# Holding w_out and moving g in a fused attention and two-MLP kernel on one Trainium2 core, with three shifts of side work

## The chip, the cores and the metric

One core of a Trainium2 (trn2) chip runs the whole program; the other cores are idle. The metric is the device time of one execution in microseconds. TensorE is written PE in the profile, and its weight loads PEld; VectorE is DVE, ScalarE is ACT, GpSimd is POOL, and SP is the engine whose queue issues nearly all DMAs.

## The reference

Attention with keys and values pooled by eight, then a gated MLP, then an MLP with a squared ReLU:

```python
k_p = k.reshape(B, H, Sp, 8, D).mean(axis=3); v_p = v.reshape(B, H, Sp, 8, D).mean(axis=3)
x = softmax(q @ k_p.T / sqrt(D)) @ v_p          # 8 x 8 heads, 576 queries, 72 pooled keys, D = 64
x = x.transpose(0, 2, 1, 3).reshape(4608, 512)
x = ((x @ w1) * (x @ w2)) @ w3 @ w_out1         # 512 -> 1024 -> 1024 -> 512
g = maximum(x @ w_in, 0) ** 2                   # 512 -> 2048
out = g @ w_out                                 # 2048 -> 512, float32
```

The inputs and weights are 8-byte floats in memory, and the kernel joins the two words of each weight into a float32.

## The kernel before, in words

Every product is made in three passes: each operand is split in a high and a low fp32r part (`hi` by ACT, `lo` by DVE), and high x high, high x low and low x high are added in PSUM. The program has these stages.

- **Fold** (`fold`): w3 @ w_out1 is folded into one matrix `W`, in groups of rows of w3. Beside it, attention tasks begin, called from `tick`, which stands between matmuls and runs a list of pumps. One pump is `attend`, the attention itself; another, `load_back`, loads k, v and q in pieces.
- **First MLP** (`stage_ab`, `stage_w`): nine blocks of 512 tokens, interleaved with the attention of later tokens. The first 512 columns of w1 and w2 stay in SBUF (`wt`). The second 512 columns are prepared by `second_half` (load, join, `hi`, `lo`, four stores), kept in a DRAM scratch as units of 256 KB (`u_w`) and fetched again for each block through a ring of eight tiles (`un`, `fetch`, L222). The pump `feed_w12` runs one step of that preparation at each tick; it is put on the list after the fold, and `stage_ab(0, 3)` waits until all steps have been issued.
- **Second MLP in pairs of blocks**: blocks are taken two at a time by a 2x2 block scheme with seven products in place of eight (Strassen's, in Winograd's form). An `h_step` (224 of them: 4 pairs x 8 units x 7 products) makes x @ w_in: six matmuls 128x512, a weight unit `un` held and the split x moved (`x2o`). An `o_step` (224 as well) makes g @ w_out. Before, it holds 128 tokens of the split g (`gt`) and moves 256 columns of w_out: twelve matmuls 128x256. The sums of an `o_step`'s product `m` are gathered in PSUM (`ob`) over eight units `u`, then added into SBUF tiles at the last unit; after products 3, 4, 5 and 6 one quarter of the pair's output is complete and is stored (`finish`, `store_out`).
- **Last block**: `ph_step` (16) and `po_step` (16) make the ninth block without the seven-product scheme.

The order of h and o steps is written by `plan`: the h steps of a pair are interleaved with the o steps of the pair before it, after a head of twelve o steps alone (`HEAD`), with a count of SBUF slots for g (`SLOTS`, `MORE`). `o_prep` splits g for an o step three o steps ahead, and it may also first replace g by a difference of two g's (L1026); the `gt` tiles are three buffers, so the split for o step k begins when o step k - 3 is done. The x of the next pair is split by `operands_of`: seven closures `cut` (B11, T1, T2, T3, B21, B22, T4, in this order; the T's with a subtraction first), which the main loop calls at marked steps (`todo_x`). The engines' final order is set by a scheduler at build time, and each engine then runs its own list in order.

The quarters of the weights w_in and w_out (`make_quarters`) are made once beside the first MLP and kept as units in DRAM.

Of the kernel before, what the change touches and what calls it, by code (L numbers as in the profile page):

```python
# [29 lines left out]
def attn_moe_moe2_kernel(  # L30
# [560 lines left out]
    def fold():  # L591
# [143 lines left out]

    def make_quarters(load, put_part):

# [12 lines left out]
        def sums(half):  # L750
            w = st_["w"]
            if half == 0:
                st_["s"] = prep_p.tile([P, 2, TB], F32, tag="w", name="sq")
            s_ = st_["s"]
            a11, a21 = w[:, 0, :PC], w[:, 0, PC:]
            a12, a22 = w[:, 1, :PC], w[:, 1, PC:]
            if half == 0:
                nc.vector.tensor_add(s_[:, 0, :PC], a21, a22)
                nc.vector.tensor_sub(s_[:, 0, PC:], s_[:, 0, :PC], a11)  # L759
            else:  # L760
                nc.vector.tensor_sub(s_[:, 1, :PC], a11, a21)
                nc.vector.tensor_sub(s_[:, 1, PC:], a12, s_[:, 0, PC:])

# [6 lines left out]
        def hi(n):  # L770
            st_["o", n] = t = prep_p.tile([P, 2, TB], F32R, tag="w", name="oq")
            nc.scalar.copy(t[:, 0, :], part(n))

        def lo(n):
            t = st_["o", n]
            nc.vector.tensor_sub(t[:, 1, :], part(n), f32(t[:, 0, :]))

# [14 lines left out]
    def in_quarters(kd, c):  # L792
# [13 lines left out]

        return make_quarters(load, put_part)

    def out_unit(key):
        return key.rearrange("p a b c -> p (a b c)").rearrange("p (i c) -> p i c", i=2)  # L810

    def out_quarters(u):
# [4 lines left out]
        return make_quarters(  # L817
            lambda x: load64(w_out[(u + x * NU) * P:(u + x * NU + 1) * P, :], raw_p), put_part)

# [17 lines left out]


    SLOTS, MORE = 38, 8

# [10 lines left out]
    def plan():  # L851
# [3 lines left out]
        free = [SLOTS]  # L855
        rest = [0]

        def out_step(todo):
            _, p, m, u = step = todo.pop(0)
            seq.append(step)  # L860
            free[0] += m in (2, 4, 5, 6)
            if u == NU - 1:
                new = (2, 2, 4, 0, 0, 0, 0)[m]
                free[0] += (0, 0, 0, 2, 2, 2, 2)[m] - new
                rest[0] -= new
            assert free[0] >= 0

        for p in range(len(pairs) + 1):
            todo = [("o", p - 1, m, u) for m in range(7) for u in range(NU)] if p else []
            if p == 1:  # L870
                free[0] += MORE
            rest[0] = 8 if p else 0
            n_o = len(todo)
# [7 lines left out]
            for x, step in enumerate(hs):  # L881
                need = step[0] == "ph" or step[3] >= 3
                while free[0] - rest[0] < need:
                    out_step(todo)
# [145 lines left out]

    def store_out(t, blk, x, half):

        r0 = blk * TB + x * 2 * P
        nc.sync.dma_start(
            out[r0:r0 + 2 * P, half * PC:(half + 1) * PC].rearrange("(t p) c -> p t c", p=P),
            t.rearrange("p (t c) -> p t c", t=2))

    def o_step(p, m, u):
# [4 lines left out]
        gt = gts.pop(("o", p, m, u))  # L1043
        for o in range(NT_):
            ps = ob[x][o // 2][:, o % 2 * PC:(o % 2 + 1) * PC]
            os_ = slice(o * P, (o + 1) * P)
            todo = [(gt[:, 0, os_], un[:, 0]), (gt[:, 0, os_], un[:, 1]), (gt[:, 1, os_], un[:, 0])]
            for j, (l, r) in enumerate(todo):
                nc.tensor.matmul(  # L1049
                    ps, l, r, start=u == 0 and m != 5 and o % 2 == 0 and j == 0,  # L1050
                    stop=u == NU - 1 and j == 2,
                    skip_group_check=True)
        fetch()
# [7 lines left out]

        def new(name, src, b):
            t = take((name, b))
            nc.vector.tensor_add(t, ob[x][b], gs[src, b])

        def add(name, b):
            nc.vector.tensor_add(gs[name, b], ob[x][b], gs[name, b])

        def finish(name, b, blk, half):
            add(name, b)  # L1070
            store_out(gs[name, b], blk, b, half)
            drop((name, b))

        for b in range(2):
            if m == 0:
                nc.scalar.copy(take(("x1", b)), ob[x][b])
            elif m == 1:
                new("x5", "x1", b)
            elif m == 2:
                new("x7", "x1", b)  # L1080
                new("x8", "x5", b)
            elif m == 3:
                add("x7", b)
                finish("x8", b, iB, 1)
            elif m == 4:
                finish("x7", b, iA, 1)
            elif m == 5:
                finish("x5", b, iB, 0)
            else:
                finish("x1", b, iA, 0)  # L1090

    def po_step(i, u):
# [6 lines left out]
        for o in range(NT_):  # L1099
# [8 lines left out]
            if u == U2 - 1:  # L1108
                st = tmp_p.tile([P, DM], F32, tag="cg", name="st2", bufs=3)
                if o % 2:  # L1110
                    nc.vector.tensor_copy(st, acc[o])
                else:
                    nc.scalar.copy(st, acc[o])
                r0 = i * TB + o * P
                nc.sync.dma_start(out[r0:r0 + P, :], st)
# [4 lines left out]
    def start_attention():  # L1120
# [3 lines left out]
        rate[0] = 0.7  # L1124


    setup_consts()
    fold()
    until(lambda: tokens_ready(TB))
    rate[0] = 0.6  # L1130

    def second_half(nm_, w, kc):
# [18 lines left out]
        def put():  # L1151
            for u in range(TB // P, U1):
# [5 lines left out]
    fh1 = merge([second_half(nm_, w, kc) for nm_, w in (("w1", w1), ("w2", w2))  # L1158
                 for kc in range(KD)], 2)
    feeds = []  # L1160
    second = []

    def feed_w12():
        if fh1:
            run_step(fh1)

# [18 lines left out]
    rate_q = [3]  # L1185
    pumps.extend([feed_w12, feed_quarters, begin_second, feed_operands])
    for i in range(NB):
# [47 lines left out]

    halves(more)
    for _ in range(U1):
# [19 lines left out]
    for step in order:  # L1257
        if step[0] == "h":
# [16 lines left out]
        else:  # L1275
            if step[:3] == ("o", 0, 0) and step[3] == 0:
                while quarters:
                    run_step(quarters)
                for _ in range(MORE // 2):
                    halves(prep_p.tile([P, 2, TB], F32, tag="w", name="gs"))  # L1280
# [39 lines left out]
```

## Time and profile before

| | us |
|---|---|
| median of 3 runs (1600.09 to 1604.88) | 1601.07 |
| the profiled execution, its own time | 1605.63 |
| its span in the profile | 1603.8 |
| PE busy in the span | 1531.9 (96%) |
| DVE busy | 975.5 (61%) |
| ACT busy | 786.4 (49%) |

The profile's page gives busy times of whole engines, the span in 40 equal slices (40.1 us each) with a digit for the busy tenths, the DMA queues, and the chain of work that ended last. A busy time is an average over stages: what a change in one stage is worth is read in that stage. The span is 1.8 us shorter than the profiled execution's own time.

### The profile page before, as it was taken

What the parts mean: (1) busy time and instruction counts of PE and PEld (TensorE: products, weight loads), DVE (VectorE), ACT (ScalarE), POOL (GpSimd) and SP (SyncE); (2) the same over time, 40 slices, a digit from 0 to 9 for tenths busy, and PEclk for the clock granted to TensorE, in tenths of its full rate; (3) what the DMA queues carried; (4) which work ended last, traced back from release to release, by engine and by line L of the source; (5) the groups of instructions that cost most, each with busy time, mean ns of one, the idle gap of its engine ahead of it and who ended that gap; (6) DMA issues with size and microseconds to landing.
All of it is one profiled execution on the core that took longest, in us unless ns stands there. A gap on an engine that the chain in (4) does not pass through costs nothing.

```text
span 1603.8 us, 24613 instructions
## 1 busy us (share of the span) xinstructions
PE 1531.9 (96%) x8288; PEld 1285.4 (80%) x8288; DVE 975.5 (61%) x1762; ACT 786.4 (49%) x1905; POOL 81.8 (5%) x146
## 2 busy tenths in 40 slices
PE   6788699999999999999999999999999999999998
PEld 3346488687878778787888889889989998999998
DVE  7688556574757467576335457648764876475432
ACT  5576434444454354546233565446454645454431
POOL 1011101111101001011000000000000000000000
PEclk9899799999999999999999999999999999999999
DMA  8454684656566575658517767777776776676764
GB/s 269 135 171 133 164 263 135 175 162 182 162 190 192 155 229 172 176 167 283 162 66 251 206 194 238 194 207 220 233 199 201 215 213 201 199 214 188 212 210 151
DMA packets 277853, 308.25 MB, mean 192 GB/s; under 512 B 98272, under 2 KB 163808, under 8 KB 277728
## 3 DMA queue, kind: packets, MB, share of 16 engines
q1 hardware_dynamic: 272544, 297.23, 62.9%
q10 hardware_dynamic: 5184, 9.44, 1.7%
q8 instruction: 67, 1.10, 0.3%
q14 instruction: 58, 0.48, 0.1%
HBM read 247.46 MB, written 56.62 MB: 190 GB/s over the span
## 4 chain that ended last, share of the span: by engine, by line
PE 53%; DVE 0%; ACT 0%; DMA 0%; issue 0%; DVEq 0%; ACTq 0%
PE o L1049 20%; PE ps_a L961 6%; PE ps_d L961 5%; PE ps_c L961 5%; PE ps_w L183 5%; PE acc L183 3%; PE ps_h L183 3%; PE o L1105 3%; PE ps_b L961 3%; PE ps_av L183 0%; DMA out_dram<-st 0%; DVE sq L759 0%; PE ps_s L414 0%; ACT att L431 0%; PE ps_t L461 0%
## 5 line engine op out<-in xcount | busy, mean ns | idle before, releaser
L1049 PEld LDWEIGHTS o<-un,gt 128*128 128x128 f32 x2688 | 342.2, 191 | 12.0
L1049 PE MATMUL o<-un,gt 128*128 128x256 f32 x2688 | 345.7, 283 | 0.0
L114 DVE TENSOR_TENSOR gt<-gs,gt 128x512 fp32r<-128x512 f32 x221 | 151.9, 689 | 194.3 <-ACT gt L113 193.9
L183 PE MATMUL ps_w<-x,wt 128*128 128x512 f32 x864 | 223.4, 401 | 4.0 <-ACT x L492 2.1
L183 PE MATMUL acc<-gt,Wt 128*128 128x512 f32 x864 | 222.3, 399 | 3.7 <-ACT st L720 2.6
L183 PE MATMUL ps_w<-x,un 128*128 128x512 f32 x864 | 215.4, 400 | 6.7 <-DMA un<-u_w 6.7
L113 ACT CAST gt<-gs 128x512 fp32r<-128x512 f32 x221 | 136.2, 616 | 153.8 <-PE o L1049 122.0
L183 PEld LDWEIGHTS ps_w<-x,un 128*128 128x128 f32 x864 | 162.4, 191 | 42.0 <-DMA un<-u_w 8.7
L183 PEld LDWEIGHTS acc<-gt,Wt 128*128 128x128 f32 x864 | 159.4, 190 | 37.1 <-ACT st L720 4.1
L183 PEld LDWEIGHTS ps_w<-x,wt 128*128 128x128 f32 x864 | 157.4, 189 | 38.6 <-DVE x L495 4.1
L431 ACT ACTIVATE att<-ps_s,mx 128x72 f32<-128x72 f32 (+1 forms) x320 | 97.9, 320 | 53.0 <-DVE mx L429 52.9
L968 ACT ACTIVATE r<-r 128x512 f32<-128x512 f32 x96 | 60.6, 632 | 121.4 <-DVE r L998 121.1
L961 PE MATMUL ps_a<-x2o,un 128*128 128x512 f32 x384 | 98.8, 392 | 0.0
L961 PE MATMUL ps_d<-x2o,un 128*128 128x512 f32 x384 | 98.4, 391 | 0.0
L961 PE MATMUL ps_c<-x2o,un 128*128 128x512 f32 x384 | 98.4, 391 | 0.0
L692 DVE TENSOR_TENSOR gf<-asb,ps_w 128x512 f32<-128x512 f32 x72 | 49.2, 683 | 78.8 <-PE ps_w L183 77.0
L113 ACT CAST gt<-gf 128x512 fp32r<-128x512 f32 x72 | 44.8, 622 | 87.1 <-DVE gf L692 81.5
L969 ACT ACTIVATE gs<-r 128x512 f32<-128x512 f32 x137 | 85.6, 630 | 3.3 <-DMA out_dram<-gs 0.6
L688 ACT COPY asb<-ps_w 128x512 f32<-128x512 f32 x72 | 42.4, 589 | 89.9 <-PE ps_w L183 89.3
L961 PEld LDWEIGHTS ps_c<-x2o,un 128*128 128x128 f32 x384 | 69.8, 189 | 12.9
L961 PEld LDWEIGHTS ps_d<-x2o,un 128*128 128x128 f32 x384 | 69.8, 189 | 12.9
L961 PEld LDWEIGHTS ps_a<-x2o,un 128*128 128x128 f32 x384 | 69.1, 189 | 12.1
(115 smaller groups left out, 2018.2 us busy)
## 6 DMA issues: line engine op xcount, KB each, us to landing
un<-u_w SPq DMA_DIRECT2D x144, 256.0 KB
un<-u_A SPq DMA_DIRECT2D x128, 256.0 KB
un<-u_S SPq DMA_DIRECT2D x128, 256.0 KB
un<-u_oA SPq DMA_DIRECT2D x128, 256.0 KB
un<-u_oS SPq DMA_DIRECT2D x128, 256.0 KB
raw<-in_moe_w_dram SPq DMA_DIRECT2D x32, 512.0 KB
raw<-in_moe_w_out_dram SPq DMA_DIRECT2D x24, 512.0 KB
x2d<-st ACTq DMA_DIRECT2D x36, 256.0 KB
```

Source lines behind the costliest of these rows:

```text
L113: nc.scalar.copy(hi, src)
L114: (eng or nc.vector).tensor_sub(lo, src, f32(hi))
L183: (lambda a=a, b=b, i=i: nc.tensor.matmul(ps, a, b, start=first and i == 0, stop=last and i == n - 1))
L431: nc.scalar.activation(av[:, h0 + h], sv[:, h], ACTF.Exp, bias=mx[:n, h:h + 1], scale=scale, accum_out=sm[:n, h0 + h:h0 + h + 1])
L688: nc.scalar.copy(asb, ps)
L692: nc.vector.tensor_mul(gf, asb, pss[1])
L961: nc.tensor.matmul(ps, l, r, start=first and j == 0, stop=j == len(todo) - 1, skip_group_check=True)
L968: nc.scalar.activation(t, src, ACTF.Relu)
L969: nc.scalar.activation(take(name), t, ACTF.Square)
L1049: nc.tensor.matmul(ps, l, r, start=u == 0 and m != 5 and o % 2 == 0 and j == 0, stop=u == NU - 1 and j == 2, skip_group_check=True)
L1105: nc.tensor.matmul(acc[o][:, y * PC:(y + 1) * PC], l, r, start=u == 0 and y == 0 and j == 0, stop=u == U2 - 1 and j == 2, skip_group_check ...
```

## The change

It has these parts.

1. `o_step` holds w_out (128 of its 256 columns as the stationary operand) and moves all 512 tokens of g: six matmuls 128x512 in place of twelve 128x256. The product then lies in PSUM transposed (columns on partitions, tokens along the row).
2. The sums of a pair are kept in four tiles of 128x1024 (`sums_o`) instead of slots of the g pool; `finish` turns a finished quarter with DVE's 32x32 transpose (128x1024) into a fifth tile and stores it by four DMAs whose runs are 64 columns (256 bytes) long; before, two DMAs stored it with runs of 256 columns (1 KB). So that the 32x32 transposes suffice, the columns of w_out's quarters are laid out in another order (`by_x`, `natural`, `quarter`), and `po_step` undoes it at its copy out of PSUM.
3. `plan` counts slots for g alone (36 of them).
4. `feed_w12` is put on the pump list in the fold's last group, where it runs at every second tick, and then at each tick. The split second half is written into the tile that the raw words were in (`raw`), instead of a tile of its own.
5. The splits for the next pair: five of the seven `cut`s are called after products 1, 3, 4, 5 and 6 of the pair's last h unit, the other two after o steps (0, 2) and (0, 5) of the head. Before, three were called after products 2, 4 and 6, and four in the head, after every third o step.

```diff
+            if nxt == U1:
+                pumps.append(feed_w12)
...
-    SLOTS, MORE = 38, 8
+    SLOTS = 20 + 2 * U1
...
-        for o in range(NT_):
-            ps = ob[x][o // 2][:, o % 2 * PC:(o % 2 + 1) * PC]
+        for o in range(2):
             os_ = slice(o * P, (o + 1) * P)
-            todo = [(gt[:, 0, os_], un[:, 0]), (gt[:, 0, os_], un[:, 1]), (gt[:, 1, os_], un[:, 0])]
+            todo = [(un[:, 0, os_], gt[:, 0]), (un[:, 0, os_], gt[:, 1]), (un[:, 1, os_], gt[:, 0])]
...
+        def add(to, src):
+            for o in range(2):
+                ps = ob[x][o].rearrange("p (j a) -> p j a", a=32)
+                nc.vector.tensor_add(sub(sums_o[to], o), ps, sub(sums_o[src], o))
+
+        def finish(name, blk, half):
+
+            add(name, name)
+            r = sums_o[4]
+            nc.vector.transpose(r, sums_o[name])
+            for i in range(P // 32):
+                c0 = i * P + half * 64
+                nc.sync.dma_start(
+                    out[blk * TB:(blk + 1) * TB, c0:c0 + 64].rearrange("(j a) c -> a j c", a=32),
+                    r[i * 32:(i + 1) * 32].rearrange("p (j c) -> p j c", c=64))
...
         def hi():
-            st_["t"] = t = prep_p.tile([P, 2, TB], F32R, tag="w", name="wt")
+
+            st_["t"] = t = st_["r"].bitcast(F32R).rearrange("p c t -> p (c t)").rearrange(
+                "p (y c) -> p y c", y=2)
             nc.scalar.copy(t[:, 0, :], st_["w"])
...
+    def feed_w12():
+        if fh1 and (folded or ticks[0] % 2 == 0):
+            run_step(fh1)
...
-            if u == NU - 1 and n in (2, 4, 6):
+            if u == NU - 1 and n in (1, 3, 4, 5, 6) and todo_x:
                 todo_x.pop(0)()
                 head = n == 6
...
-            if todo_x and head and n_out % 3 == 0:
+            if todo_x and head and step[2:] in ((0, 2), (0, 5), (1, 1), (1, 3)):
                 todo_x.pop(0)()
```

Three places show how the engines' lists move. The first is PE's list in the second MLP, at product 6 of the first pair's o steps (`o` is the PSUM sum of an o step, `ps_b` to `ps_d` are those of the h steps). Before:

```order
L1049 MATMUL o_9096<-un,gt_10541 128x256 x6
L1049 MATMUL o_9097<-un,gt_10541 128x256 x6
L961 MATMUL ps_b<-x2o,un 128x512 x6
L1049 MATMUL o_9096<-un,gt_10582 128x256 x6
L1049 MATMUL o_9097<-un,gt_10582 128x256 x6
```

Now:

```order
L1052 MATMUL o_9098<-gt_10254,un 128x512 x3
L1052 MATMUL o_9099<-gt_10254,un 128x512 x3
L965 MATMUL ps_b<-x2o,un 128x512 x6
L1052 MATMUL o_9098<-gt_10289,un 128x512 x3
L1052 MATMUL o_9099<-gt_10289,un 128x512 x3
```

The steps stand in the same order here; each o step has half the matmuls, of twice the length.

The second place is DVE's list where the second pair's o steps go from product 0 to product 1 (`gt_N` is the low part of one o step's g, `gs<-gs` one difference of two g's made ahead of its o step, `u` and `r` are sums of the h steps). Before:

```order
L114 TENSOR_TENSOR gt_10979<-gs,gt_10979 128x512
L1026 TENSOR_TENSOR gs<-gs 128x512 x2
L114 TENSOR_TENSOR gt_11003<-gs,gt_11003 128x512
L1026 TENSOR_TENSOR gs<-gs 128x512
L114 TENSOR_TENSOR gt_11021<-gx,gt_11021 128x512
L1026 TENSOR_TENSOR gs<-gs 128x512 x2
L114 TENSOR_TENSOR gt_11050<-gs,gt_11050 128x512
L1026 TENSOR_TENSOR gs<-gs 128x512 x2
L989 TENSOR_TENSOR u_11062<-ps_b,p_11047 128x512
L1026 TENSOR_TENSOR gs<-gs 128x512 x3
```

Now:

```order
L114 TENSOR_TENSOR gt_10599<-gs,gt_10599 128x512
L1030 TENSOR_TENSOR gs<-gs 128x512
L114 TENSOR_TENSOR gt_10611<-gs,gt_10611 128x512
L1030 TENSOR_TENSOR gs<-gs 128x512 x13
L114 TENSOR_TENSOR gt_10623<-gs,gt_10623 128x512
L1030 TENSOR_TENSOR gs<-gs 128x512 x2
L114 TENSOR_TENSOR gt_10646<-gs,gt_10646 128x512
L1030 TENSOR_TENSOR gs<-gs 128x512 x2
L993 TENSOR_TENSOR u_10658<-ps_b,p_10643 128x512
```

The differences, which stood by ones to threes between the `gt`s, stand thirteen in a row between the `gt` of o step (1, 4) and that of (1, 5). The same block of thirteen stands at the third pair, and one of eight at the fourth.

The third place is SP's list at the end of the fold, from the first raw load of a second half (`raw`; `u_w` are the stores of its split parts, `kv<-in_v` the loads of the second batch's v, `vl` and `vr` the placing of v in the layout that attention reads). Before:

```order
L290 DMA kv<-in_v_dram 128x512
L125 DMA raw<-in_moe_w_dram 128x1024
L290 DMA kv<-in_v_dram 128x512 x2
L125 DMA raw<-in_moe_w_dram 128x1024
L290 DMA kv<-in_v_dram 128x512
L293 DMA kv<-in_v_dram 16x512 x4
L125 DMA raw<-in_moe_w_dram 128x1024
L207 DMA u_w_4_0_1226<-wt 128x2x128
...
L125 DMA raw<-in_moe_w_dram 128x1024
L333 DMA vl<-vhl 72x4x64 x2
L333 DMA vl<-vhl 56x4x64 x2
L337 DMA vr<-vhl 16x64 x12
```

Now:

```order
L125 DMA raw<-in_moe_w_dram 128x1024
L288 DMA kv<-in_k_dram 64x512
L125 DMA raw<-in_moe_w_dram 128x1024 x2
L207 DMA u_w_4_0_1138<-raw 128x2x128
...
L290 DMA kv<-in_v_dram 128x512
L222 DMA un<-u_w_4_0_1138 128x512
...
L125 DMA raw<-in_moe_w_dram 128x1024 x2
L333 DMA vl<-vhl 72x4x64 x2
L333 DMA vl<-vhl 56x4x64 x2
L337 DMA vr<-vhl 16x64 x12
```

The raw loads move ahead of the loads of v: seven of the eight now stand ahead of `vr`, where four did, and the first load of v stands behind the eight stores of the first two second halves.

## Rows read from the trace of the kernel before

**Rows 1.** The page's slices (PE busy, granted clock), 40 of 40.1 us each.

```profile
PE   6788699999999999999999999999999999999998
...
PEclk9899799999999999999999999999999999999999
```

**Rows 2.** Busy time by stretch: start:end, length, busy (instructions), clock, DMA share, GB/s.

```profile
160.00:200.00 40.00, 25.15 (x115) 18.93 (x114) 21.02 (x51) 20.16 (x76) 5.28 (x9) 0.79 0.60 160
400.00:500.00 100.00, 96.87 (x463) 77.24 (x462) 64.42 (x135) 47.45 (x165) 11.73 (x21) 0.98 0.65 186
955.00:1555.00 600.00, 600.00 (x3909) 549.74 (x3908) 380.51 (x594) 310.03 (x526) 0.00 (x0) 1.00 0.72 209
```

**Rows 3.** The chain that ended last, in time: start, length, what.

```profile
882.27 2.72 PE acc L183 x12
955.71 17.27 PE o L1049 x144
...
1553.22 43.93 PE o L1105 x366
```

**Rows 4.** PE's timeline in the second MLP: start, length, instructions.

```profile
952.82 1.52 PE L961 MATMUL ps_c<-x2o,un 128*128 128x512 f32 x6
954.18 1.52 PE L961 MATMUL ps_d<-x2o,un 128*128 128x512 f32 x6
...
1035.94 1.60 PE L1049 MATMUL o<-un,gt 128*128 128x256 f32 x12
1037.38 1.55 PE L961 MATMUL ps_c<-x2o,un 128*128 128x512 f32 x6
1038.76 1.60 PE L1049 MATMUL o<-un,gt 128*128 128x256 f32 x12
```

**Rows 5.** The costliest groups, shapes apart: busy, mean ns | idle before.

```profile
L1049 PE MATMUL o<-un,gt 128*128 128x256 f32 x2688 | 345.7, 283 | 0.0
L1049 PEld LDWEIGHTS o<-un,gt 128*128 128x128 f32 x2688 | 342.2, 191 | 12.0
...
L392 DVE STREAM_TRANSPOSE qT<-qraw 128x320 f32<-128x320 f32 x24 | 12.1, 506 | 0.2
...
L392 DVE STREAM_TRANSPOSE qT<-qraw 128x256 f32<-128x256 f32 x24 | 10.2, 432 | 4.8 <-DMA qraw<-in_q_dram 4.8
```

**Rows 6.** ACT's timeline in the first head: start, length, what [idle, releaser].

```profile
964.38 0.62 ACT L113 CAST gt<-gs 128x512 fp32r<-128x512 f32 x1 [0.82 <-PE o L1049]
```

**Rows 7.** DVE's timeline behind that head.

```profile
979.25 1.88 DVE L1026 TENSOR_TENSOR gs<-gs 128x512 f32<-128x512 f32 x3
981.05 0.68 DVE L114 TENSOR_TENSOR gt<-gs,gt 128x512 fp32r<-128x512 f32 x1
```

**Rows 8.** PE's timeline behind the fold.

```profile
158.45 0.62 PE L183 MATMUL ps_av<-aT,vl 128*128 128x256 f32 x3
...
196.79 1.17 PE L183 MATMUL ps_av<-aT,vl 128*128 128x320 f32 x3 [2.32 <-ACT att L431]
...
201.20 19.40 PE L183 MATMUL ps_w<-x,un 128*128 128x512 f32 x72 [2.97 <-DMA un<-u_w]
```

**Rows 9.** SP's DMA queue behind the fold: start, time to issue, what.

```profile
127.65 0.33 SPq L290 DMA_DIRECT2D kv<-in_v_dram  x1
...
142.61 2.12 SPq L207 DMA_DIRECT2D u_w<-wt  x4
...
162.04 0.49 SPq L125 DMA_DIRECT2D raw<-in_moe_w_dram  x1
...
177.09 0.49 SPq L125 DMA_DIRECT2D raw<-in_moe_w_dram  x1
...
198.34 3.87 SPq L222 DMA_DIRECT2D un<-u_w  x8
```

**Rows 10.** DMA packets, in 955:1555 and then in 400:500.

```profile
DMA packets 72123, 125.44 MB, mean 209 GB/s; under 512 B 7584, under 2 KB 15264, under 8 KB 72073
...
DMA packets 31177, 18.64 MB, mean 186 GB/s; under 512 B 16577, under 2 KB 25261, under 8 KB 31168
```

More of the change, by code (lines that the diff above doesn't have):

```diff
@@ L732, in attn_moe_moe2_kernel, with make_quarters @@
     PC = 2 * P
-    def make_quarters(load, put_part):
+    def make_quarters(load, put_part, quarter, order=lambda t: t, natural=lambda t: t):
         st_ = {}
@@ L771, in hi @@
             st_["o", n] = t = prep_p.tile([P, 2, TB], F32R, tag="w", name="oq")
-            nc.scalar.copy(t[:, 0, :], part(n))
+            nc.scalar.copy(order(t[:, 0, :]), natural(part(n)))
         def lo(n):
             t = st_["o", n]
-            nc.vector.tensor_sub(t[:, 1, :], part(n), f32(t[:, 0, :]))
+            nc.vector.tensor_sub(
+                order(t[:, 1, :]), natural(part(n)), order(f32(t[:, 0, :])))
         def put(n):
@@ L817, in out_quarters @@
         return make_quarters(
-            lambda x: load64(w_out[(u + x * NU) * P:(u + x * NU + 1) * P, :], raw_p), put_part)
+            lambda x: load64(w_out[(u + x * NU) * P:(u + x * NU + 1) * P, :], raw_p), put_part,
+            lambda t, x, y: t[:, x].rearrange("p (i y z) -> p i y z", i=4, y=2)[:, :, y, :],
+            by_x, natural)
     quarters = merge(
@@ L855, in plan @@
         free = [SLOTS]
-        rest = [0]
         def out_step(todo):
@@ L882, in plan @@
                 need = step[0] == "ph" or step[3] >= 3
-                while free[0] - rest[0] < need:
+                while free[0] < need:
                     out_step(todo)
@@ L1029, in o_prep, with sub @@
         gts[step] = gt
[L1031 to L1036, printed above, removed]
+    sums_o = []
+    def sub(t, x):
+        return t.rearrange("p (j x a) -> p j x a", x=2, a=32)[:, :, x, :]
     def o_step(p, m, u):
@@ L1060, in o_step @@
         iA, iB = pairs[p]
[L1062 to L1090, printed above, removed]
+        def add(to, src):
[11 more added lines that the diff above has]
+                    r[i * 32:(i + 1) * 32].rearrange("p (j c) -> p j c", c=64))
+        if m == 0:
+            for o in range(2):
+                nc.scalar.copy(sub(sums_o[0], o), ob[x][o].rearrange("p (j a) -> p j a", a=32))
+        elif m == 1:
+            add(1, 0)
+        elif m == 2:
+            add(2, 0)
+            add(3, 1)
+        elif m == 3:
+            add(2, 2)
+            finish(3, iB, 1)
+        elif m == 4:
+            finish(2, iA, 1)
+        elif m == 5:
+            finish(1, iB, 0)
+        else:
+            finish(0, iA, 0)
     def po_step(i, u):
@@ L1124, in start_attention @@
         rate[0] = 0.7
[L1127 to L1130, printed above, removed]
     def second_half(nm_, w, kc):
@@ L1159, in attn_moe_moe2_kernel @@
                  for kc in range(KD)], 2)
+    def feed_w12():
+        if fh1 and (folded or ticks[0] % 2 == 0):
+            run_step(fh1)
+    folded = []
+    setup_consts()
+    fold()
+    folded.append(True)
+    until(lambda: tokens_ready(TB))
+    rate[0] = 0.6
     feeds = []
     second = []
-    def feed_w12():
-        if fh1:
-            run_step(fh1)
     def feed_quarters():
@@ L1185, in attn_moe_moe2_kernel @@
     rate_q = [3]
-    pumps.extend([feed_w12, feed_quarters, begin_second, feed_operands])
+    pumps.extend([feed_quarters, begin_second, feed_operands])
     for i in range(NB):
@@ L1234, in halves @@
         slots.extend(t[:, x] for x in range(2))
-    halves(more)
+    sums_o.append(more.rearrange("p x c -> p (x c)"))
     for _ in range(U1):
@@ L1278, in attn_moe_moe2_kernel @@
                     run_step(quarters)
-                for _ in range(MORE // 2):
-                    halves(prep_p.tile([P, 2, TB], F32, tag="w", name="gs"))
+                for _ in range(4):
+                    t = prep_p.tile([P, 2, TB], F32, tag="w", name="so")
+                    sums_o.insert(0, t.rearrange("p x c -> p (x c)"))
             prepare()
             n_out += 1
-            if todo_x and head and n_out % 3 == 0:
+            if todo_x and head and step[2:] in ((0, 2), (0, 5), (1, 1), (1, 3)):
                 todo_x.pop(0)()
```

37 lines of the change are left out of this document (17 added, 20 removed).

## The prediction

> **What bounds the kernel now.** The profiled execution took 1605.63 us, its span 1603.8, with 1.8 around it. That is 4.56 us above the median of the runs (1601.07), so I make the sum against 1605.63 and take 4.56 off at the end.
>
> I read the slices first [rows 1]: PE's digits are below 9 only in the first six, the fold and the attention's start, and the granted clock is lowest there too. Then the busy time by stretch [rows 2]: from 955 to 1555 us PE is busy 600.0 of 600 us at clock 1.00, DVE 380.5, ACT 310.0, and the DMA engines 0.72. So the second MLP is bound by PE alone: a microsecond saved there on PE is one off the end until another engine takes over, and work of other engines there costs only by making PE wait. In 160 to 200 us PE is busy 25.15 of 40: the one gap that is worth anything. The chain in time [rows 3] and PE's timeline [rows 4] give the price of a step, the groups [rows 5] that of a transpose, ACT's and DVE's timelines [rows 6, 7] how g is split, and the rest [rows 8 to 10] the gap behind the fold and the DMA packets.
>
> **Part 1: o_step holds w_out.** The head's twelve o steps are 144 matmuls of 128x256 in 17.27 us [rows 3]: 119.9 ns each, 1.44 us a step. The page's means for one matmul [rows 5] overlap, so I use starts. An h step, six matmuls of 128x512, takes 954.18 - 952.82 = 1.36 us [rows 4], and twelve such matmuls take 2.72 us also where split activations are the moving operand, as in the change (`acc`) [rows 3]: 226.7 ns each. Two short ones cost 239.8, so a merged pair saves 13.1 ns. There are 224 x 12 / 2 = 1344 pairs: 17.6 us. The stretch with o steps goes from 955.71 to 1553.22, 597.5 us [rows 3], and holds 224 o steps, 168 h steps and 16 ph steps of twelve 128x512 matmuls. At the long matmul's price that is (224 + 168) x 1.36 + 16 x 2.72 = 576.6 us, 20.9 less. The other 3.3 us are partly the change of form between steps, which vanishes too: an h step before an o step takes 1038.76 - 1037.38 = 1.38 us [rows 4]. I take **-20.9**; the ends are -17.6 and -20.9, and 0 if the saving per matmul isn't there (a rival). The weight loads halve; at 191 ns each [rows 5] beside a matmul of 226.7 they stay hidden. The last 384 short matmuls (po_step) keep their form.
>
> A difference of 239.8 - 226.7 means a fixed 13.1 ns for each matmul, and 106.8 ns for every 256 columns. The Trainium skill, TensorE: Matmul & The Clock Gate, on the back-to-back gap, gives a fixed cost of about 2.5 ns for each warm matmul; by that, as an estimate, part 1 would save only 1344 x 2.5 = 3.4 us. The rows here show five times that cost, in both forms.
>
> **Part 2: sums and stores.** The adds are as many as before. New on DVE are 16 transposes of 128x1024. From 506 ns for 320 elements and 432 for 256 [rows 5] comes 1.156 ns an element, so 1.32 us each, 21 us in all. DVE rises to about 402 us of a stretch of 579 (69%), beside PE: 0, but for what is said of the head below. A finish stores 2048 runs of 256 bytes in place of 512 of 1 KB; 16 finishes write 32,768 packets in place of 8192. No row has a price for such a packet alone. In the second MLP one takes 0.72 x 600 us x 16 / 72123 = 96 ns for 1.74 KB on average, in 400 to 500 us 0.65 x 100 x 16 / 31177 = 33 ns for 598 bytes [rows 2, 10]. By bytes alone a 256-byte packet would take 14 ns; at 33 I take the nearest row. Then the share rises by at most 32,768 x 33 ns / 16 / 579 = 12%, less about 5% for the 8192 packets of 1 KB that go (56 ns each, by bytes from the 96): 0.72 to 0.79. One finish gives each engine 128 packets, 4.3 us. Weight units come through a ring of eight: a fetch is issued seven steps of 1.36 us ahead of its use, 9.5 us, and needs 201.20 - 198.34 = 2.9 to land [rows 8, 9]. 6.6 us of slack cover 4.3: **0**.
>
> The Trainium skill, DMA: Bandwidth & Descriptors, in its table of specifications, puts the smallest transfer at line rate at 512 bytes, with a read-modify-write below. It speaks against these stores; the rival on stores below says from which price a packet would decide.
>
> **Part 3: plan.** The slots only shift which h and o steps are neighbours: **0**, PE has the same steps and both forms now cost the same. But where o steps shift, DVE's list does too. Between the gt's of o steps (1, 4) and (1, 5) DVE now has thirteen differences in a row; before, three at most. Three and the start of the next work take 1.80 us [rows 7]: 0.60 each, 7.8 in all. ACT's split of an o step starts when the o step three before ends (955.71 + 6 x 1.44 = 964.35, ACT starts at 964.38 [rows 6]). So from the end of (1, 1), DVE needs 7.8 + about 1.3 for the split before (0.62 [rows 6] and 0.68 [rows 7]) + 0.68 for the next = 9.8 us, while PE has six steps, 8.2 us. PE then waits about 1.7 us, at pairs 2 and 3, and about 1 for the block of eight at the fourth: 4.4.
>
> **Part 5: splits of x in the head.** Five of seven now lie among the h products, where o steps have gt's split ahead. Twelve lows, two adds, six operations for the two cuts left in the head and at least four differences are 24 at a pitch of 0.60 us [rows 7], 14.4, and with a transpose 15.7 us of DVE, against 12 x 1.36 = 16.3 us of PE. Before, PE had 17.3 us for a head and never waited [rows 3]. It is a near thing with three o steps of lead, and I take 1.2 us for each of three heads: 3.6. Together **+8**; the ends are 0 (DVE's neighbours give way) and +14 (each head loses twice that, each block its own double).
>
> **Part 4: the second halves earlier.** In the gap, attention work ends at 196.79 + 1.17 = 197.96, and the products with `un` start at 201.20, behind a fetch issued at 198.34, when the last stores have been issued [rows 8, 9]. The raw loads behind 160 us come some 5 us apart (162.04 to 177.09, four of them): the preparation of the second halves fills that time. With three of these loads moved ahead, up to 15 us of it is gone, and all the idle time of 160 to 200 us is 40 - 25.15 = 14.85 [rows 2]. Against it: SP's queue is in order, and the first load of v, at 127.65 before [rows 9], now stands behind eight stores, the like of which were issued at 142.61, when their low part was ready. If the split is no earlier than that, v comes up to 15 us later, and with it vr, and the attention whose first products with v stood at 158.45 [rows 8]. But part 4 begins that preparation some 30 ticks earlier, in the fold, so part of the wait is gone. Ends -15 and +14; the chain of attention, which sets the end today at 197.96, isn't shortened, so I take a small **-2**.
>
> **Sum.** -20.9 + 0 + 8 - 2 = -14.9: 1605.63 to 1590.7, in terms of the median 1601.07 - 14.9 = **1586**. A measurement of this kernel can tell about 0.3%, 4.8 us, from no change.
>
> **The rivals.**
>
> The gap behind the fold goes and DVE keeps up: fold -12, DVE +5, PE -20.9: 1573. For it speaks that SP's queue holds the last fetch back [rows 9]; against, that attention ended only 0.4 us before that fetch.
>
> The fold gets later and DVE binds: +8 (half of the v loads' 15) and +12: 1600, no change. For it: the row at 142.61, and the DVE block of thirteen. Against: both together are needed.
>
> Slower, by the 256-byte stores. PE waits when a finish holds the fetches of the ring longer than their slack of 6.6 us: from 6.6 / 128 = 52 ns a packet. At twice the row's 33 ns, 8.4 us a finish, each of 16 costs 1.8 us, +29: 1615. The kernel gets slower than before from 6.6 + 14.9 / 16 = 7.5 us a finish, 59 ns a packet. Against it: even packets under 2 KB, among them many below 512 bytes, came to 33 ns on average [rows 10].
>
> The change doesn't do what it says: the fixed part per matmul stays with the step (with its weights or its start), and twelve or six cost the same 1.44 us: 0 + 8 - 2, 1607, no change or slower. Against it: the six matmuls of an h step and the twelve of `acc` both give 226.7. The page on TensorE above would bring it to -3.4 + 8 - 2 = +2.6, about 1604.
>
> **How the numbers follow.** Forecast 0.58 (its own range 1578 to 1594: -17.6 + 14 - 2 above, -20.9 + 0 - 2 below); gap gone 0.21; fold later 0.11; stores 0.06; no saving 0.04. Faster takes the first two, 0.79; same the third and the last, 0.15; slower the stores, 0.06. The range 1572 to 1599 leaves out the half of the fold rival, the stores and the last, and the best cases of a gap gone and DVE free.
>
> **What would show it.** An o step's pitch of 1.36 us, and its group of 128x512 matmuls near 1344 x 227 ns = 305 us where 345.7 stood [rows 5] (the mean counts overlap, so starts decide). PE idle ahead of o step (1, 5) at pairs 2 and 3, released by DVE's gt. The first product with `un` against 201.20, and the first of attention with v against 158.45. A DMA share up to 0.79 and no wait of PE for `un` behind a finish. I'm wrong if PE in the second MLP waits over 10 us for DVE or DMA, if an o step still takes 1.44 us, or if the gap at 200 us moves by over 5.

## The result and the profile after

The changed kernel takes 1583.91 us (median of 4 runs, 1582.54 to 1586.48) where the kernel before takes 1602.3 on the same chip: the ratio is 0.9887, with a 95% interval of 0.9864 to 0.9909. That is 18.4 us faster, where 14.9 was forecast. The profiled execution of the change took 1585.05 us, its span is 1583.2.

The second MLP is read first, since three of the four terms of the sum lie there. The first row is the stretch from the first o step to the place where the po steps begin in the chain of waits, as in [rows 3]; the second is the stretch behind the fold, as in [rows 2]:

```profile
947.34:1532.68 585.34, 580.45 (x2547) 476.57 (x2546) 394.06 (x606) 305.54 (x524) 0.00 (x0) 1.00 0.74 213
...
160.00:200.00 40.00, 29.59 (x129) 22.35 (x128) 21.66 (x51) 19.62 (x69) 4.99 (x9) 0.76 0.61 162
```

Before, the o steps began at 955.54 us and the po steps at 1553.22, 597.68 us. Now it is 585.34: 12.3 us less there, and the o steps begin 8.2 us earlier; together that is 20.5 of the 20.6 us by which the spans differ. PE, which had no idle time in this stretch before, now has 4.9 us of it, and DVE's busy time rose to 394 of 585 us. The groups of o_step on the page:

```profile
L1052 PE MATMUL o<-gt,un 128*128 128x512 f32 x1344 | 330.8, 390 | 4.9 <-DVE gt L114 4.5
L1052 PEld LDWEIGHTS o<-gt,un 128*128 128x128 f32 x1344 | 251.3, 188 | 61.2 <-DVE gt L114 9.0
```

There are half as many matmuls as in [rows 5]. Their busy time, 330.8 us, counts what overlaps, so starts decide here too. And now they wait: 4.9 us in all, 4.5 of it for the low part of a `gt` from DVE. PE's timeline where the second pair's head ends shows one of those waits:

```profile
1118.38 1.52 PE L965 MATMUL ps_a<-x2o,un 128*128 128x512 f32 x6
1119.74 1.52 PE L965 MATMUL ps_b<-x2o,un 128*128 128x512 f32 x6
1121.10 1.52 PE L1052 MATMUL o<-gt,un 128*128 128x512 f32 x6
1122.46 1.52 PE L965 MATMUL ps_c<-x2o,un 128*128 128x512 f32 x6
1123.82 0.39 PE L1052 MATMUL o<-gt,un 128*128 128x512 f32 x1
1125.82 1.45 PE L1052 MATMUL o<-gt,un 128*128 128x512 f32 x5 [1.62 <-DVE gt L114]
1127.11 1.54 PE L965 MATMUL ps_d<-x2o,un 128*128 128x512 f32 x6
```

An o step and an h step now have the same pitch, 1.36 us (1122.46 - 1121.10). O step (1, 5) begins its first matmul at 1123.82, and its second, the first that needs the low part, starts 2.00 us later, where one matmul takes 0.23: 1.77 us are lost. DVE's timeline at the same place tells why:

```profile
1116.66 0.68 DVE L114 TENSOR_TENSOR gt<-gs,gt 128x512 fp32r<-128x512 f32 x1
1117.27 7.90 DVE L1030 TENSOR_TENSOR gs<-gs 128x512 f32<-128x512 f32 x13
1125.09 0.68 DVE L114 TENSOR_TENSOR gt<-gs,gt 128x512 fp32r<-128x512 f32 x1
```

The thirteen differences take 1125.09 - 1117.27 = 7.82 us, and the low part that PE wants stands behind them. The chain of waits goes through them, and through the eight at the fourth pair:

```profile
1117.34 7.83 DVE gs L1030 x13
...
1272.98 7.83 DVE gs L1030 x13
...
1427.86 4.82 DVE gs L1030 x8
...
1532.68 43.93 PE o L1112 x366
```

Ahead of the second MLP, SP's queue behind the fold (compare [rows 9]):

```profile
128.70 3.36 SPq L125 DMA_DIRECT2D raw<-in_moe_w_dram  x2
...
137.34 4.10 SPq L207 DMA_DIRECT2D u_w<-raw  x8
141.60 0.37 SPq L290 DMA_DIRECT2D kv<-in_v_dram  x1
...
194.37 3.87 SPq L222 DMA_DIRECT2D un<-u_w  x6
```

The first load of v stands behind the eight stores, at 141.60 in place of 127.65, and the fetch of the weight units comes at 194.37 in place of 198.34. PE's timeline (compare [rows 8]):

```profile
167.92 2.88 PE L183 MATMUL ps_w<-x,un 128*128 128x512 f32 x12
...
170.87 0.63 PE L183 MATMUL ps_av<-aT,vl 128*128 128x256 f32 x4
...
200.63 0.47 PE L479 MATMUL ps_av<-aR,vr 96*128 96x320 f32 x1
200.90 15.14 PE L183 MATMUL ps_w<-x,un 128*128 128x512 f32 x60
```

Twelve matmuls with `un` now lie ahead of the gap; the second batch's attention starts later (its first products with v at 170.87, before at 158.45), and the long run of products starts at 200.90, as before at 201.20. What it waits for has changed: before, attention had ended 3 us earlier and the products waited 2.97 us for the fetch of `un` [rows 8]; now they stand right behind the last product of attention, with no wait.

The stores of the finishes: the DMA view of the o stretch, first before, then after.

```profile
DMA packets 71897, 125.04 MB, mean 209 GB/s; under 512 B 7552, under 2 KB 15232, under 8 KB 71847
...
q1 hardware_dynamic: 71847, 124.37, 71.7%
```

```profile
DMA packets 95361, 124.75 MB, mean 213 GB/s; under 512 B 38756, under 2 KB 38756, under 8 KB 95323
...
q1 hardware_dynamic: 95323, 124.27, 73.6%
```

Packets took 0.717 x 597.68 x 16 = 6857 us of the engines before and 0.736 x 585.34 x 16 = 6893 after, though there are 31,200 more short ones and 7,680 fewer of 1 KB. At the 56 ns of the prediction the latter were 430 us, so 31,200 short ones cost about 466: 15 ns each. One execution isn't enough for this: in the runs below with the same stores the packets took 6817 to 6995 us (ahead1, late_again), and in early_only, which stores as before, 6749 (70.6% of 597.51 us). That makes it 12 to 22 ns, an estimate that rests on the 56. That range takes in the price by bytes (14), and not the 33 ns of the nearest row.

### The profile page after: what moved, and what is told of

It reads as the page before. It is cut to its first block, busy times and chain, and to the rows that moved or that the text cites. A ratio compares the mean times of both kernels' runs of the same rounds, so it can differ in the third digit from the quotient of the medians.

```text
span 1583.2 us, 21959 instructions
## 1 busy us (share of the span) xinstructions
PE 1514.2 (96%) x6944; PEld 1215.8 (77%) x6944; DVE 992.7 (63%) x1778; ACT 784.0 (50%) x1905; POOL 83.9 (5%) x146
## 4 chain that ended last, share of the span: by engine, by line
PE 78%; DVE 10%; DMA 4%; ACT 4%; SPq 3%; issue 2%; DVEq 0%; ACTq 0%
PE ps_w L183 23%; PE o L1052 14%; PE acc L183 11%; PE ps_a L965 5%; PE ps_c L965 5%; PE ps_d L965 5%; PE o L1112 3%; PE ps_h L183 3%; PE ps_b L965 2%; DVE gs L1030 2%; PE ps_s L414 2%; DVE gt L114 2%; PE ps_av L183 1%; DMA raw<-in_moe_w_dram 1%; PE ps_w L641 1%
## 5 line engine op out<-in xcount | busy, mean ns | idle before, releaser
L1052 PE MATMUL o<-gt,un 128*128 128x512 f32 x1344 | 330.8, 390 | 4.9 <-DVE gt L114 4.5
L1052 PEld LDWEIGHTS o<-gt,un 128*128 128x128 f32 x1344 | 251.3, 188 | 61.2 <-DVE gt L114 9.0
L114 DVE TENSOR_TENSOR gt<-gs,gt 128x512 fp32r<-128x512 f32 x240 | 163.8, 687 | 186.2 <-ACT gt L113 185.9
L113 ACT CAST gt<-gs 128x512 fp32r<-128x512 f32 x240 | 148.5, 619 | 164.0 <-PE o L1052 111.2
L183 PE MATMUL acc<-gt,Wt 128*128 128x512 f32 x864 | 218.8, 396 | 0.0
L973 ACT ACTIVATE gs<-r 128x512 f32<-128x512 f32 x144 | 89.5, 629 | 1.6
L1030 DVE TENSOR_TENSOR gs<-gs 128x512 f32<-128x512 f32 x128 | 83.6, 683 | 2.0 <-ACT gs L973 0.7
L965 PEld LDWEIGHTS ps_c<-x2o,un 128*128 128x128 f32 x384 | 71.9, 188 | 15.7 <-DVE u L996 0.9
```

The costliest lines, as they stand in the source:

```text
L113: nc.scalar.copy(hi, src)
L114: (eng or nc.vector).tensor_sub(lo, src, f32(hi))
L183: (lambda a=a, b=b, i=i: nc.tensor.matmul(ps, a, b, start=first and i == 0, stop=last and i == n - 1))
L965: nc.tensor.matmul(ps, l, r, start=first and j == 0, stop=j == len(todo) - 1, skip_group_check=True)
L973: nc.scalar.activation(take(name), t, ACTF.Square)
L1030: nc.vector.tensor_sub(src, a, src)
```

## The experiments

All runs of a line of this table were timed beside the kernel before on one chip; the runs were made in three groups (late_w12 to pinned, ahead1 to stores128, the last three), and the median of before was 1601.49, 1602.74 and 1602.9 us in them. The first o step and the stretch from it to the first po step are from one profiled execution each, and both go by the start of the first matmul in PE's timeline, which for the po steps lies 0.16 us ahead of the place in the chain.

| run | median us | ratio to before (95%) | first o step | o stretch |
|---|---|---|---|---|
| before | 1602.3 | | 955.54 | 597.51 |
| the change | 1583.91 | 0.9887 (0.9864 to 0.9909) | 947.34 | 585.17 |
| late_w12 | 1590.06 | 0.9930 (0.9913 to 0.9947) | 950.17 | 585.19 |
| early_only | 1597.38 | 0.9970 (0.9959 to 0.9980) | 948.93 | 597.51 |
| mm256 | 1605.77 | 1.0030 (1.0021 to 1.0039) | 944.98 | 607.39 |
| pinned | 1586.87 | 0.9907 (0.9891 to 0.9922) | 946.96 | 587.88 |
| ahead1 | 1580.49 | 0.9852 (0.9831 to 0.9872) | 949.05 | 579.70 |
| old_cuts | 1584.79 | 0.9886 (0.9868 to 0.9904) | 949.04 | 585.14 |
| wt_tile | 1583.19 | 0.9879 (0.9861 to 0.9897) | 946.93 | 585.22 |
| stores128 | 1585.84 | 0.9893 (0.9876 to 0.9910) | 948.95 | 585.23 |
| after_again | 1583.73 | 0.9879 (0.9861 to 0.9898) | 948.39 | 585.29 |
| late_again | 1589.70 | 0.9920 (0.9899 to 0.9940) | 949.88 | 585.24 |
| ahead_old | 1577.34 | 0.9834 (0.9815 to 0.9854) | 946.27 | 578.39 |

The last column repeats within 0.15 us where a kernel's second MLP is the same (585.17 to 585.29 in six executions, stores128 among them). The column ahead of it doesn't: with the same first part it runs from 944.98 to 949.05. So the second MLP can be read from one profile, and what lies ahead of it only from medians of times.

**mm256** gives each matmul of an o step half the columns again and leaves the roles as in the change.

```diff
-                nc.tensor.matmul(ob[x][o], l, r, ...)
+                for y in range(2):
+                    ys = slice(y * PC, (y + 1) * PC)
+                    nc.tensor.matmul(ob[x][o][:, ys], l, r[:, ys], ...)
```

> The change with each 128x512 matmul of an o step made as two of 128x256 (same weights held, two halves of g moved). Theory (each matmul has a fixed part of 13.1 ns): an o step takes 1.44 us again, 224 x 6 x 13.1 ns = 17.6 us more, about 1600. Rival (what was saved belongs to the roles, to what is held and what is moved, or to the weight load): an o step stays at 1.36 us and the time at 1584. A fixed part of 2.5 ns would give 3.4 us, 1587.

The o stretch is 22.2 us longer than in the change. PE's timeline of mm256 away from the heads:

```profile
1001.11 1.59 PE L1054 MATMUL o<-gt,un 128*128 128x256 f32 x12
1002.54 1.55 PE L965 MATMUL ps_c<-x2o,un 128*128 128x512 f32 x6
1003.92 1.59 PE L1054 MATMUL o<-gt,un 128*128 128x256 f32 x12
```

An o step takes 1.43 us and an h step ahead of an o step 1.38, as before in [rows 4], against 1.36 and 1.36 in the change: 0.09 us for each of 224 o steps, 20.2 us. The rest is losses at single places. Against before, whose steps it repeats, mm256 loses 9.9 us, most of it at three waits (PE is idle for 7.0). At the third pair, after 3.15 us of that, the granted clock fell to 0.52 and 0.62 (1290 to 1294 us), which cost about 1.5. The change loses 8.6 (below). Without both, the two kernels differ by 22.2 - 9.9 + 8.6 = 20.9 us. The theory counted 17.6, without the change of form; so its time, about 1600, was too low for the 1605.77 measured. The price goes with the number of matmuls and with the change of form between steps, not with which operand is held: in this the first theory holds. The fixed part is what [rows 3] gave, about 13 ns a matmul. One thing is not separated: each matmul has its own weight load, in mm256 too (2688), so the 13 ns may belong to the load as well as to the matmul, and the rival's weight load is not excluded.

**pinned** and **ahead1** move the differences on DVE's list. In pinned each stays where the program writes it, ahead of its own split; in ahead1 it is written one o step earlier, ahead of the split before, and stays there in the same way.

```diff
-                nc.vector.tensor_sub(src, a, src)
+                tc.keep_in_program_order(nc.vector.tensor_sub(src, a, src))
```

> The change with each difference of two g's kept in program order on DVE, right ahead of its o step's split, so that there are no rows of 13 and 8. Theory (the waits at pairs 2, 3 and 4 come from those rows): PE's waits for DVE's gt behind the heads (1.77, 1.74 and 0.44 us, with the slower matmuls after them about 4.9) go, 1579. Rival (DVE is short of time there, whatever the order): PE waits as long, in other places, 1583 to 1586.

The long waits went, and the stretch became 2.7 us longer all the same. DVE's timeline in the first head of pinned:

```profile
960.49 0.69 DVE L114 TENSOR_TENSOR gt<-gs,gt 128x512 fp32r<-128x512 f32 x1 [1.09 <-ACT gt L113]
961.09 0.68 DVE L1030 TENSOR_TENSOR gs<-gs 128x512 f32<-128x512 f32 x1
962.52 0.69 DVE L114 TENSOR_TENSOR gt<-gs,gt 128x512 fp32r<-128x512 f32 x1 [0.74 <-ACT gt L113]
963.13 0.69 DVE L1030 TENSOR_TENSOR gs<-gs 128x512 f32<-128x512 f32 x1
```

A low part every 962.52 - 960.49 = 2.03 us, with DVE idle 0.74 in each: the difference waits behind the low part before it, ACT's high part for the difference, the low part for ACT. This chain, not DVE's busy time, is slower than PE's 1.36 us wherever o steps stand close together. By the starts of PE's matmuls it costs 0.8 us in the first head, and 2.3, 2.3 and 1.5 at the later ones, where the rows of differences had cost 2.2, 2.2 and 0.6. Neither the theory nor the rival had it. The rival's 1583 to 1586 is close to the time, but not for its reason, since DVE sits idle in every step of the chain: the row of differences was a wait, and its removal made another.

The second edit is that of ahead1; `o_diff` is the subtraction of pinned, taken out of `o_prep`.

```diff
...
+            while n_diff[0] < min(n_prep[0] + 1 + 1, len(outs)) and ready(outs[n_diff[0]]):
+                o_diff(outs[n_diff[0]])
+                n_diff[0] += 1
             o_prep(outs[n_prep[0]])
```

> The change with each difference of two g's made one o step ahead of its split, in program order on DVE: neither thirteen in a row nor, as in the run pinned, each right ahead of its own split. Theory (PE waits where DVE's list holds a gt back, by a row of differences or by a chain of high part, low part, difference and next high part of 2.05 us an o step): both waits go, the stretch of the o steps is 580 to 581 us in place of 585.3, and the time 1579 to 1580. Rival (DVE has too little time in and behind the heads in any order): 585, the time 1584 or more.

It came out as the theory had it: 579.70 us in place of 585.17, and 1580.49. DVE does the same work (397.6 us busy in the stretch), so it wasn't short of time behind the heads; its order was late.

**old_cuts** calls the splits of the next x at the places of before.

```diff
-            if u == NU - 1 and n in (1, 3, 4, 5, 6) and todo_x:
+            if u == NU - 1 and n in (2, 4, 6):
...
-            if todo_x and head and step[2:] in ((0, 2), (0, 5), (1, 1), (1, 3)):
+            if todo_x and head and n_out % 3 == 0:
```

> The change with the splits of the next x called as before (three after h products 2, 4 and 6, four in the head after every third o step). Theory of the prediction (DVE has 15.7 of 16.3 us of work in a head): six operations more in each of the heads make it 3 us short in three or four heads; PE waits 6 to 12 us more, 1590 to 1596. Rival (the three o steps of lead and the list's order absorb it): 1584 to 1586.

The stretch is 585.14, no longer than the change's, with more splits in each head. The theory, which is the prediction's reason for its 3.6 us, falls: a head isn't short of DVE time with four of them in it. What the first head of the change waited for (with the slow matmul behind it 1.3 us, at 953) is gone here; there the last lows of x stood ahead of the first `gt`s, here they stand between them.

That the two stretches are equal is chance. PE's timeline of old_cuts behind the third head, and the stretches of busy time there, whose third number from the end is the granted clock:

```profile
1281.84 2.16 PE L1052 MATMUL o<-gt,un 128*128 128x512 f32 x5 [1.79 <-DVE gt L114]
1283.80 2.41 PE L965 MATMUL ps_d<-x2o,un 128*128 128x512 f32 x6
```

```profile
1282.00:1284.00 2.00, 2.00 (x6) 1.56 (x7) 2.00 (x4) 0.00 (x0) 0.00 (x0) 0.56 0.32 123
1284.00:1286.00 2.00, 2.00 (x6) 1.57 (x6) 1.99 (x4) 0.62 (x1) 0.00 (x0) 0.58 0.48 110
```

Behind PE's wait of 1.79 us the clock fell to its lower level, 1.2 GHz, for most of these 4 us, and matmuls of 0.227 us took 0.427: seven of them, 1.4 us. A wait of 1.78 us at the second pair left the clock at 1.00. So the old places gained in the first head what this execution lost to the clock: the new places of part 5 cost 1.3 us there, and nothing shows that they gained.

**ahead_old** joins ahead1 and old_cuts.

> The change with the differences one o step ahead and the splits of x called as before. The run ahead1 left one wait of 1.0 us at the first head and 0.9 us in each of the next two; in old_cuts the first was gone. Theory (the first head's wait comes from three lows of x that stand ahead of the first gt's): the o stretch is 578.3 to 579 us in place of 579.7. Rival: with both, the heads are short of DVE time again, and it is 580 or more. In the time the two can't be told apart: 1579 to 1581.

578.39 us, 1.3 less than ahead1: the first head's wait is gone, as the theory had it, and 0.9 and 0.8 us are left in the second and the third head. PE's weight loads in the second head of the change show what those are, and DVE's timeline the reason:

```profile
1104.22 1.23 PEld L1052 LDWEIGHTS o<-gt,un 128*128 128x128 f32 x6 [0.53 <-DVE gt L114]
1105.95 6.23 PEld L1052 LDWEIGHTS o<-gt,un 128*128 128x128 f32 x28 [0.50 <-DVE gt L114]
```

```profile
1102.30 1.27 DVE L1067 TENSOR_TENSOR so<-o,so 128x512 f32<-128x512 f32 x2
1103.50 0.67 DVE L114 TENSOR_TENSOR gt<-gs,gt 128x512 fp32r<-128x512 f32 x1
1104.10 1.23 DVE L1073 STREAM_TRANSPOSE gx<-so 128x1024 f32<-128x1024 f32 x1
1105.26 1.25 DVE L114 TENSOR_TENSOR gt<-gs,gt 128x512 fp32r<-128x512 f32 x2
```

The two waits lie behind the two adds and behind the transpose of the last finish of the pair before, which DVE does ahead of the low parts of the head. This place was read, not tested by a run. At 1577.34 us ahead_old beats both kernels; against after_again on the same chip it is 6.4 us faster.

**late_w12**, **early_only**, **after_again** and **late_again** are about part 4. late_w12 takes it out of the change, early_only puts it alone into the kernel before; late_again and after_again repeat the pair on one chip. The edit of late_w12 and late_again:

```diff
-            if nxt == U1:
-                pumps.append(feed_w12)
...
-            st_["t"] = t = st_["r"].bitcast(F32R)...
+            st_["t"] = t = prep_p.tile([P, 2, TB], F32R, tag="w", name="wt")
...
-    pumps.extend([feed_quarters, begin_second, feed_operands])
+    pumps.extend([feed_w12, feed_quarters, begin_second, feed_operands])
```

> The change without its part 4: the second halves are begun after the fold and split into a tile of their own, as before. Theory (the whole gain ahead of the second MLP, 955.54 to 947.34 us = 8.2, comes from part 4): the first o step starts at 955 to 956 us again, and the time is 1592 (8 above the change). Rival (the forecast's term was right at 2, and some 6 us come from other work that the change moved or from chance in the first MLP): the first o step starts near 949 to 950, and the time is 1586.

> The kernel before with part 4 alone. Theory: the first o step starts near 947.3 us instead of 955.5 and the time is 1594 (8 below before); the stretch of the o steps keeps its 597.7 us. Rival: 1600, with the first o step at 953 or later.

> The changed kernel itself, beside late_again on one chip, since executions of one kernel reach the first o step at times that differ by up to 4 us and part 4's worth is of that size. Theory (part 4 is worth the 4 to 6 us that the two earlier pairs of medians give): late_again is 4 to 6 us slower than this run. Rival (the forecast's term of 2 was right): 2 us or less between them. Second rival (the 8.2 us between the two profiles is the worth): 8.

> The change without its part 4, as in late_w12, on the chip of after_again: 1588 to 1590 by the theory, 1586 by the rival, 1592 by the second rival.

By the medians part 4 is worth 1601.49 - 1597.38 = 4.1 us in the kernel before and 1589.70 - 1583.73 = 6.0 in the change: the theory of the last pair, between the forecast's 2 and the 8.2 that the two profiles show. The interval of early_only alone, 3.2 to 6.6 us, leaves out both 2 and 8. The first theory, all of 8.2, falls by these medians. The first o steps alone can't tell: late_w12 starts them at 950.17 and not at 955 to 956, though PE's list is that of before up to there. The profiled execution of before lay 3.3 us above the median of its runs in the result and that of late_w12 2.2 below its own, and the 5.4 us between them are no more than that.

Where the 4 to 6 us lie shows in part in the stretches of PE's busy time, much the same in every execution with part 4 (27.9 to 30.2 us in the gap, 199.8 to 200.0 from 500 to 700) and in every one without (24.6 to 26.2, and 194.0 to 194.1). late_again and then after_again, 160 to 200 and 500 to 700 us:

```profile
160.00:200.00 40.00, 24.61 (x115) 18.31 (x115) 20.80 (x50) 19.98 (x75) 5.29 (x9) 0.79 0.64 175
...
500.00:700.00 200.00, 193.97 (x926) 156.91 (x925) 127.45 (x259) 93.09 (x301) 19.25 (x34) 1.00 0.63 183
```

```profile
160.00:200.00 40.00, 27.90 (x131) 20.75 (x130) 23.23 (x53) 21.77 (x79) 4.99 (x9) 0.86 0.65 178
...
500.00:700.00 200.00, 199.87 (x963) 163.57 (x962) 127.45 (x264) 94.27 (x305) 22.59 (x35) 1.00 0.63 184
```

PE is busy 3.3 us more in the gap, and 5.9 more from 500 to 700 us, where it now hardly waits; from 300 to 500 it gives 3.2 back (191.43 in place of 194.65). In the gap the granted clock is 0.79 and 0.86, so that busy time there is worth less than elsewhere. So the early second halves gain something near the forecast's 2 at the gap, and shift the attention of the later batches against the products, which gains as much again. Why those later waits go was not tried, and stays open.

**wt_tile** keeps the early start and gives the split its own tile again.

```diff
-            st_["t"] = t = st_["r"].bitcast(F32R)...
+            st_["t"] = t = prep_p.tile([P, 2, TB], F32R, tag="w", name="wt")
```

> The change with the split second halves in tiles of their own as before (the pump still in the fold's last group). Theory (those four tiles hold w_out1 until the fold's last products, so the stores can't start earlier, and the early start is worth little without the raw tile): the 30 or so matmuls with un ahead of 200 us go, and the time is 1587 to 1590. Rival (loads and joins are what had to be early; v's first load no longer stands behind eight stores, so attention is earlier): 1582 to 1585.

1583.19, as the rival had it: the stores start at 138.94 (137.34 in the change) all the same, and v's first load at 136.84 is ahead of them. The early start is what counts; the raw tile isn't needed for it. The theory's sign did come: wt_tile has no matmul with `un` ahead of 198.92 us, where the change has twelve. The time is the same, so those twelve aren't what part 4 gains.

**stores128** cuts the finishes' stores in halves of 128 bytes.

```diff
-                c0 = i * P + half * 64
-                nc.sync.dma_start(...)
+                for y in range(2):
+                    c0 = i * P + half * 64 + y * 32
+                    nc.sync.dma_start(...)
```

> The change with the finishes' stores cut in runs of 128 bytes, eight DMAs each. Theory (a packet costs by its bytes, 15 ns for 256 bytes as the change of the DMA share says): the share in the o stretch stays at 0.74, 1584. First rival (a packet costs at least 15 ns, however short): 30,720 more packets take 29 us of each of 16 engines, the share is 0.79, one finish 3.8 us, within the ring's slack of 6.6: 1584. Second rival (short packets cost far more than 15 ns): above 26 ns one finish passes the slack, PE waits for un; at 33 ns 1.8 us x 16, 1613. SP issues four more DMAs of 0.45 us at each finish: nothing, if the slack holds.

The DMA view of its o stretch:

```profile
DMA packets 127043, 124.78 MB, mean 213 GB/s; under 512 B 70432, under 2 KB 70432, under 8 KB 127004
...
q1 hardware_dynamic: 127004, 124.28, 74.1%
```

31,700 more packets, and the share is within the 73.0 to 74.7% of the kernels that have the same stretch without them: against the lowest, wt_tile, 102 us more (6938 - 6836), 3 ns a packet. The theory holds, both rivals fall, and PE waits for no `un`.

## Why the prediction was right

- **Part 1**, -20.9 us: right in size and reason. 597.51 us became 585.17 with 8.6 us of losses in it (585.17 - 576.6), and 578.39 in ahead_old, where only 1.7 us of waits are left: 576.7 without them, as the sum at the long matmul's price had it. mm256 gives it back. The Trainium skill, TensorE: Matmul & The Clock Gate, on the back-to-back gap, gives a fixed cost of about 2.5 ns for each warm matmul. The rows and mm256 give 13.1 ns, five times that, and the measurement decides.
- **Parts 3 and 5**, +8: 8.6 was lost. The blocks of thirteen and eight were forecast at 4.4 and cost about 2.2, 2.2 and 0.6: the wait itself (1.7 forecast, 1.77 and 1.74 measured) and 0.5 behind it, while DVE catches up (PE's weight loads for `ps_c` then wait 0.4 for DVE's `u`). The heads were forecast at 3.6 and cost 1.3, 1.0 and 1.0. That this size fits is luck, for here the step that failed is the reason, "a near thing" between 15.7 us of DVE and 16.3 of PE: old_cuts has more of this work and loses less in the heads. What costs is which instruction stands ahead of a low part: three lows of x in the first head (ahead_old), an add and a transpose in the others (read, not tested). ahead1 shows that the blocks cost what was lost behind the heads; that part 3 is what made the blocks was not tried.
- **Part 2**, 0: right. The transposes take 1.236 us (1.32 forecast). The packets cost 12 to 22 ns, near the price by bytes, where the nearest row, 33, was taken; the share became 0.74, not 0.79. A finish's burst is then at most 128 x 22 ns = 2.8 us, far within the ring's slack of 6.6. The Trainium skill, DMA: Bandwidth & Descriptors, in its table of specifications, puts the smallest transfer at line rate at 512 bytes, with a read-modify-write below. At 12 to 22 ns a packet, where bytes alone make 14, these stores show no clear loss from it.
- **Part 4**, -2: the mis-sized term; it is 4 to 6. Both sides of its mechanism came as forecast: v's first load 14 us later (15 at most was said), part of the products ahead of the gap (wt_tile gains as much without them), the long run of products at 200.90, unmoved. The step that failed is that the gain was taken from the place where the gap ends, "the chain of attention, which sets the end today at 197.96, isn't shortened". The rows already said otherwise: the products waited 2.97 us for the fetch, not for attention. In the change that wait is gone, attention ends some 3 us later and takes its place as the end, PE does more within the gap, and by PE's busy time about half of the gain comes from less waiting after it, which the forecast did not look at. With 6.0 for this term and 8.6 for the one before, the terms make -18.3, where 18.4 was measured.
- **The rivals.** The gap going with DVE keeping up, 1573, came halfway: the gap's term grew, DVE's did not shrink. The price of a packet, at most 22 ns, is well below the 59 ns from which the store rival decides. That the saving isn't there is excluded by mm256. The fold did not make the products behind it later (200.90 us, before 201.20).
- The profiled execution of before lay above its median, and the sum was made in differences, so nothing of that came into the forecast; the comparison of the two profiles alone would have put 2 to 4 us too much down to part 4.
- Two slips of the working that nothing hangs on: in [rows 1] PE's digits are below 9 in the first five slices and in the last, not in the first six; and the upper end of the forecast's own range, -17.6 + 14 - 2 = -5.6, is 1595.5 and not 1594.

## What to carry to other kernels

Where PE has no idle time, the price of a step is its number of matmuls times a fixed part and its columns: take both from two forms that the trace already holds. Then look in the order listing for what stands ahead of the one small instruction that PE waits for; an engine at 67% can still hold PE up with a row of thirteen operations that nobody needs yet. Spread them, but one step ahead of their use: right at their use they make a chain through two engines.

## What was not expected of the hardware

A store's packet of 256 or of 128 bytes cost the DMA engines about as much per byte as longer ones (12 to 22 ns for 256 bytes, by bytes 14; about 3 ns or less for each packet that halving adds). The fixed part of a matmul with its weight load, about 13 ns, is the same whichever operand is held: in mm256, where two matmuls that follow each other hold the same weights (which are loaded for each, 2688 times), an o step takes what it takes with g held. And a wait of PE can cost more than its length: in old_cuts the granted clock fell behind a wait of 1.79 us, in mm256 behind one of 3.15, and 1.4 and 1.5 us more were lost, while waits as long at the second pair left the clock at 1.00.
